# Linear attention, mixture of experts and a gated layer on one core: the order of the recurrence's products changed

## The chip, the core and the metric

The kernel runs on one core of a Trainium2 chip. Its engines are TensorE (PE in the profile; its weight loads are shown apart as PEld), VectorE (DVE), ScalarE (ACT), GpSimd (POOL) and SyncE (SP, which here only issues transfers). The metric is the device time of one execution in microseconds, the median of several runs.

## The reference, cut to what matters

Three stages follow one another: a gated linear recurrence (attention), a layer of eight experts of which each token takes one, and a dense gated layer.

```python
# attention: batch 4, heads 8, 768 steps, head size 48
state = f[:, :, t, :, None] * state + einsum('bhd,bhe->bhde', k[:, :, t], v[:, :, t])
y[:, :, t] = einsum('bhd,bhde->bhe', q[:, :, t], state)      # f = sigmoid(f_logit)
# experts: 3072 tokens of 384, 8 experts of width 1024
logits = x @ w_gate + modality_bias[modality_id]
e_idx = argmax(logits, axis=1);  probs = softmax(logits)
out[mask] = gate_w[mask, None] * (maximum(x[mask] @ w1[e], 0) @ w2[e])
# gated layer of width 1536
return (sigmoid(x @ w_gate) * (x @ w_val)) @ w_out
```

## The kernel before

**Tiles.** The recurrence is cut into chunks of 128 steps. With 6 chunks and 4 batches there are 24 tiles (NT); tile i belongs to chunk i // 4 and batch i % 4, and holds all 8 heads. A loop over i from 0 to NT + 1 writes the code of several tiles in one pass: the products of tile i, the outputs of tile i - 1, the routing of tile i - 2, and the preparation of tiles i + 2 and i + 3. The schedule is written by hand (`tc.manual_schedule()`): each engine works through its instructions in the order in which this code issues them, and waits on semaphores where it needs another's result.

**The products of one pass on PE,** under the names that the profile gives to their results:

- `ktr` (line 957): four transposes of the keys of tile i. The whole array is used, 128 rows by 128 columns.
- `a` (line 969): eight products of keys and queries of tile i. Each uses 48 rows of one half of the array's rows (64 by 128); two lie side by side. DVE masks them into `am` (line 975).
- `c` (line 923): eight sums of the log gates of tile i + 2. Each uses 64 columns (128 by 64); two lie side by side. ACT makes `r` and `g` from them.
- `xtok` (line 1047): four products that turn the output of tile i - 2 into token order and give the router's logits. Whole array.
- `u` (line 987): eight products for the state's update in tile i, 128 by 64. DVE adds them to `ss` (lines 997 and 999).
- `yT` of line 1015: four products of the queries of tile i - 1 with the state, whole array. Tiles of the first chunk have none. It is called yS below.
- `yT` of line 1021: eight products of `am` and the values of tile i - 1, 128 by 64, into the same accumulation. It is called yA below. ACT copies the result to memory (line 1026).

So the array is used in three shapes: whole (F), split by rows (R: only `a`), split by columns (C: `c`, `u`, yA). A float32 product shows as two MATMUL records in the trace. In the order before, one full pass reads F R C F C F C.

**Routing.** The tiles are routed in groups (ROUTE): 0 to 3, 4 to 7, 8 to 11, 12 to 15, 16 and 17, 18 to 21, 22 and 23. When the last tile of a group has gone through `xtok`, the generator `route_a` issues the steps on DVE from logits to the one-hot choice `oh`. One pass later `att_r` issues the `rank` products on PE, which count tokens per expert, and then `route_pos` on DVE: six small steps and, for each tile, one `row` and one `place` (lines 307 and 309), here called marks. `put_table` multiplies the marks on PE and adds the result to a table on DVE (line 334). DVE's steps of these generators are issued one at a time by `tick()` between other work, or all at once by `drain()`.

**Before, a pass after the rank products** (`to_put`) the code drains the marks and then issues the `put` products, in passes 7, 11, 15 and 19. After pass 19 the routing of tiles 16 and 17 gives the tables of the first two expert slots: `early_tables` on DVE, `put` and `take` on PE in pass 21, a gather of rows, and two expert slots in float32 (`slot32`), of which the first begins in pass 25.

**Buffers.** PSUM tiles rotate: three for `a` and `c`, two (tag "o") for `u` and `yT`, two (tag "t") for `ktr` and `xtok`, one (tag "lg") for `rank`, `put` and `take`. Every fourth pass from the third on (CONV) and the pass behind it also convert a piece of the last layer's weights, on ACT and DVE.

Of the kernel before, what the change touches and what calls it, by code (L numbers as in the profile page):

```python
# [10 lines left out]
F32 = mybir.dt.float32  # L11
# [11 lines left out]
P = 128  # L23
B, H, S, D = 4, 8, 768, 48
NCH = S // P
NT = B * NCH
NTOK = B * S
DM = H * D
E = 8
# [12 lines left out]
ROUTE = ((0, 4), (4, 4), (8, 4), (12, 4), (16, 2), (18, 4), (22, 2))  # L42
CUM = len(ROUTE) % 2
CONV = (3, 7, 11, 15)
GROUP = (0, 6, 1, 2)
STAGED = (3, 7)
PADS = (320, 160, 352, 96)
# [13 lines left out]
def kernel(  # L61
# [167 lines left out]
    def drain():  # L229
        while chains:  # L230
            tick()
# [11 lines left out]
    def route_a(logits_ps, bias, n, to):  # L243
        shp = [P, n, E]
        lg = small.tile(shp, F32, tag="lg", name="lg")
        nc.vector.tensor_tensor(out=lg, in0=logits_ps, in1=bias, op=ALU.add)
        yield
        mx = small.tile([P, n], F32, tag="mx", name="mx")
        nc.vector.tensor_reduce(out=mx, in_=lg, axis=AX.X, op=ALU.max)
        yield  # L250
        nc.vector.tensor_tensor(out=lg, in0=lg, in1=bc3(mx, shp, 2), op=ALU.subtract)
        ez = small.tile(shp, F32, tag="ez", name="ez")
        nc.scalar.activation(out=ez, in_=lg, func=AF.Exp)
        yield
        sc = small.tile(shp, F32, tag="sc", name="sc")
        w8b = bc3(w8, shp, 1)
        nc.vector.scalar_tensor_tensor(out=sc, in0=lg, scalar=0.0, in1=w8b, op0=ALU.is_ge, op1=ALU.mult)
        yield
        first = small.tile([P, n], F32, tag="first", name="first")
        nc.vector.tensor_reduce(out=first, in_=sc, axis=AX.X, op=ALU.max)  # L260
        yield
        oh = small.tile(shp, BF16, tag="oh", name="oh", bufs=3)
        nc.vector.tensor_tensor(out=oh, in0=w8b, in1=bc3(first, shp, 2), op=ALU.is_equal)
        to.update(oh=oh, ez=ez)
        yield

    def route_rank(oh, c, n, count=False):
        ps = ps_t.tile([P, n + count, E], F32, tag="lg", name="rank", bufs=1)
# [53 lines left out]

    marks = []

    def put_table():

        ps = ps_t.tile([HI, 2, P], F32, tag="lg", name="put", bufs=1)
        steps = [(half, row, place) for row, place in marks for half in range(2)]
        marks.clear()
        for n, (half, row, place) in enumerate(steps):  # L330
            nc.tensor.matmul(
                out=ps[:, half], lhsT=row[:, half], rhs=place, start=(n == 0), stop=(n == len(steps) - 1)
            )
        nc.vector.tensor_tensor(out=table, in0=table, in1=ps, op=ALU.add)
# [11 lines left out]
    def route_cum(oh, c, c_new, n):  # L346
        if n > 2:
            total = small.tile([P, E], F32, tag="total", name="total")
            nc.vector.tensor_reduce(out=total, in_=oh.rearrange("p n e -> p e n"), axis=AX.X, op=ALU.add)
            yield  # L350
            nc.vector.tensor_tensor(out=cum[c_new], in0=cum[c], in1=total, op=ALU.add)
            yield
        for j in range(n if n <= 2 else 0):
            nc.vector.tensor_tensor(out=cum[c_new], in0=cum[c if j == 0 else c_new], in1=oh[:, j], op=ALU.add)
            yield
# [650 lines left out]
                at = slice(64 * j, 64 * j + D)  # L1006
                nc.scalar.copy(out=s_blk[b][at, :, at], in_=s_sum[b][at])

    def att_y(i):
        c, b = i // B, i % B  # L1010
        (am, _), qT, vt = st.pop(("am", i)), st.pop(("qT", i)), st.pop(("v", i))
        ps = ps_o.tile([P, 4, P], F32, tag="o", name="yT")
        if c:
            for pr in range(4):
                nc.tensor.matmul(
                    out=ps[:, pr, :], lhsT=s_blk[b][:, pr, :], rhs=qT[:, pr, :], start=(pr == 0), stop=False
                )
        for pr in range(4):
            for j in range(2):
                h = 2 * pr + j  # L1020
                nc.tensor.matmul(
                    out=ps[64 * j:64 * j + 64, pr, :], lhsT=vt[:, h * D:h * D + 64], rhs=am[:, 4 * j + pr, :],
                    start=(c == 0 and pr == 0), stop=(pr == 3),
                )
        yT = ap2.tile([P, 4, P], F32, tag="yT", name="yT")
        nc.scalar.copy(out=yT, in_=ps)
        st["yT", i] = yT
# [35 lines left out]
    def att_r(i):  # L1063

        drain()
        first_i, n = group_of[i]
        c = ROUTE.index((first_i, n)) % 2
        got = st.pop(("oh", first_i))
        oh = got["oh"]
        rank = route_rank(oh, c, n, i == NE - 1)  # L1070
        steps = (
            route_pos(oh, rank, n, first_i, late_at(first_i, n)),
            route_cum(oh, c, 1 - c, n), route_weight(got["ez"], st["rows", first_i], n),
        )
# [12 lines left out]
    def general(flag):  # L1087
        with tc.If(flag != 0), ExitStack() as gctx:
# [53 lines left out]
            with tc.For_i(0, NTOK, P) as r0:  # L1142
# [22 lines left out]
                    nc.tensor.matmul(out=lg[:, 0], lhsT=xt[:, c, :], rhs=wn[:, c, :], start=(c == 0), stop=(c == 2))  # L1165
                got = {}
                run(route_a(lg, bi, 1, got))
                oh, ez = got["oh"], got["ez"]
# [72 lines left out]
        for _ in steps:  # L1241
            tick()

    to_store = due = to_put = None
    for i in range(NT + 2):
        routed = due
        due = i - 2 if i >= 2 and sum(group_of[i - 2]) == i - 1 else None
# [7 lines left out]
            load_v(i + 3)  # L1255
        if to_store is not None and to_store != NE - 1:
            store_rows(to_store)
        if i < NT:
            att_k(i)
            att_a(i)  # L1260
        if to_put and to_put < NE - 1:
            drain()
            put_table()
        if i == NE + 3:
            put_table()
        if i + 2 < NT:
            prep_c(i + 2)
            prep_e(i + 2)
        if i == NE + 3:
            tabs["ids"] = take_table(tabs["esel"], "eids").rearrange("p (t s) -> p t s", t=2)  # L1270
        if routed is not None and routed < NE - 1:
            att_r(routed)
        if i < NT:
            att_m(i)
        if i == NE + 2:
            drain()
            store_rows(NE - 1)
        tick()
        if i + 3 < NT:
            prep_l(i + 3)  # L1280
        if i in CONV:
            convert_mask()
        if i == NT + 1:
            slot_0 = slot32(w0, early_x[0], hooks_0, early_cur[0])
            next(slot_0)
        if 0 <= i - 2 < NT:
            att_x(i - 2)
            if i >= NT - 1:
                drain()
        if i == NT:  # L1290
            att_r(NT - 3)
            drain()
            to_store = NT - 3
        if i == NT + 1:
            next(slot_0)
            next(slot_0)
        if i < NT:
            state = att_u(i)
            if i == 0:
                keep_warm(1)  # L1300
        if 0 <= i - 1 < NT:
            att_y(i - 1)
        if i == NT - 1:
            gps = ps_t.tile([1, P], F32, tag="lg", name="gps", bufs=1)
            nc.tensor.transpose(gps, gm1, ident)
# [12 lines left out]
        to_put = routed  # L1318
# [448 lines left out]
```

## Time and profile before

| what | value |
|---|---|
| median of 3 runs | 879.3 us (875.5 to 879.44) |
| the profiled execution | 878.71 us, span 877.0 us |
| PE busy | 853.0 us (97%) of the span |
| DVE, ACT, POOL busy | 476.8 us (54%), 389.2 us (44%), 249.8 us (28%) |
| mean granted clock of TensorE | 0.991 of full speed |
| attention, passes 2 to 24 | about 21.7 to 164.8 us of the span |
| float32 expert slots, then experts | to about 212 us, then to about 418 us |
| gated layer | to the end |

PE counts as busy while any of its products is in flight, and that time is modelled, so 97% doesn't mean that it works at its peak: what a run of products costs is read from where it starts and where the next one starts.

### The profile page before, as it was taken

The numbers are of one execution on the slowest core, as the hardware profiler recorded it, in microseconds if no ns is written. First come the engines' busy times: TensorE is split into PE (matmuls) and PEld (weight loads), VectorE is DVE, ScalarE is ACT, GpSimd is POOL, SyncE is SP. The second block draws the span as 40 slices with busy tenths as digits, with TensorE's granted clock in tenths as the row PEclk, the third lists the DMA queues.
The fourth block names the chain that finished last, engine by engine and source line by source line (L and its number), as shares of the span: only waits on it lengthen the run. The fifth ranks groups of instructions, "written<-read, shape, count | busy, mean of one in ns | idle before, by whom it ended". The sixth has DMA issues, their size and how long they took to land.

```text
span 877.0 us, 15315 instructions
## 1 busy us (share of the span) xinstructions
PE 853.0 (97%) x5802; PEld 762.9 (87%) x5802; DVE 476.8 (54%) x1036; ACT 389.2 (44%) x804; POOL 249.8 (28%) x321
## 2 busy tenths in 40 slices
PE   7999999999999999999999999999999999999995
PEld 6888888777999999999888888888888888888885
DVE  5777778475987979976335334333423433442221
ACT  5866675225866656656432322232322332223222
POOL 5744443113445665564630200020020001002002
PEclk8999999999999999999999999999999999999998
DMA  9566653864989979976202021011012002000000
GB/s 324 177 219 232 217 171 123 332 242 149 336 302 327 330 270 321 333 260 226 80 10 64 27 47 35 1 55 37 18 46 46 19 1 64 10 0 37 1 1 36
DMA packets 52273, 121.15 MB, mean 138 GB/s; under 512 B 21018, under 2 KB 33318, under 8 KB 52192
## 3 DMA queue, kind: packets, MB, share of 16 engines
q1 hardware_dynamic: 47200, 105.10, 35.6%
q0 software_dynamic: 4992, 15.00, 4.8%
q8 instruction: 47, 0.77, 0.4%
q14 instruction: 34, 0.28, 0.1%
HBM read 96.44 MB, written 20.11 MB: 133 GB/s over the span
## 4 chain that ended last, share of the span: by engine, by line
PE 69%; DVE 4%; issue 1%; ACT 1%; POOL 0%; POOLq 0%; DVEq 0%; ACTq 0%
PE gv L1595 11%; PE gv L1596 11%; PE gv L1594 11%; PE y L735 8%; PE o L1619 6%; PE o L1617 6%; PE o L1618 6%; PE h L659 3%; PE h L656 3%; PE h L657 3%; DVE cvt L850 2%; DVE al L389 1%; DVE hl L663 1%; PE xT L403 0%; DVE bl L389 0%
## 5 line engine op out<-in xcount | busy, mean ns | idle before, releaser
L1605 DVE TENSOR_TENSOR sg<-sg,gv 128x256 f32<-128x256 f32 (+1 forms) x145 | 60.2, 415 | 209.3 <-PE gv L1596 209.3
L1606 ACT CAST gh<-sg 128x256 fp32r<-128x256 f32 (+1 forms) x145 | 58.7, 405 | 191.6 <-DVE sg L1605 191.6
L1625 POOL DMA_INDIRECT out_dram<-raw,tok x24 | 23.6, 984 | 375.5 <-ACT raw L1622 369.3
L1607 DVE TENSOR_TENSOR gl<-sg,gh 128x256 fp32r<-128x256 f32 (+1 forms) x145 | 64.3, 443 | 68.2 <-ACT gh L1606 68.2
L1604 ACT ACTIVATE sg<-gv 128x256 f32<-128x256 f32 (+1 forms) x145 | 55.2, 381 | 94.7 <-PE gv L1596 92.6
L393 POOL DMA_INDIRECT xg<-xd,ids x24 | 36.5, 1523 | 62.9 <-PE xT L403 38.9
L662 ACT ACTIVATE hh<-h 128x256 fp32r<-128x256 f32 x80 | 30.9, 386 | 42.7 <-PE h L659 42.0
L663 DVE SCALAR_TENSOR_TENSOR hl<-h,hh 128x256 fp32r<-128x256 f32 x80 | 33.3, 419 | 21.8 <-ACT hh L662 18.2
L1596 PE MATMUL gv<-oddh,al 128*128 128x512 f32 (+1 forms) x120 | 44.3, 369 | 0.0
L1595 PE MATMUL gv<-oddl,ah 128*128 128x512 f32 (+1 forms) x120 | 44.3, 369 | 0.0
L1594 PE MATMUL gv<-oddh,ah 128*128 128x512 f32 (+1 forms) x120 | 44.1, 367 | 0.0
L1596 PE MATMUL gv<-oddh,bl 128*128 128x512 f32 x108 | 42.5, 394 | 0.0
L1596 PE MATMUL gv<-evenh,bl 128*128 128x512 f32 x108 | 42.5, 393 | 0.0
L1595 PE MATMUL gv<-oddl,bh 128*128 128x512 f32 x108 | 42.4, 393 | 0.0
L1595 PE MATMUL gv<-evenl,bh 128*128 128x512 f32 x108 | 42.4, 393 | 0.0
L945 POOL TENSOR_TENSOR qT<-kq,g 128x512 f32<-128x512 f32 x19 | 24.4, 1283 | 62.9 <-ACT g L935 47.8
L1596 PE MATMUL gv<-evenh,al 128*128 128x512 f32 x108 | 42.3, 391 | 0.0
L1595 PE MATMUL gv<-evenl,ah 128*128 128x512 f32 x108 | 42.2, 391 | 0.0
L1594 PE MATMUL gv<-evenh,ah 128*128 128x512 f32 x108 | 42.0, 389 | 0.0
L1594 PE MATMUL gv<-evenh,bh 128*128 128x512 f32 x108 | 42.0, 389 | 0.0
L1594 PE MATMUL gv<-oddh,bh 128*128 128x512 f32 x108 | 42.0, 389 | 0.0
L975 DVE TENSOR_TENSOR am<-a,causal 128x512 f32<-128x512 f32 x48 | 31.2, 683 | 12.5 <-PE a L969 12.5
(365 smaller groups left out, 2487.8 us busy)
## 6 DMA issues: line engine op xcount, KB each, us to landing
raw<-in_w_dram SPq DMA_DIRECT2D x48, 768.0 KB, 5.8
kq<-in_att_kq_dram SPq DMA_DIRECT2D x24, 512.0 KB, 5.4
cvr<-in_w_glu_dram SPq DMA_DIRECT2D x14, 768.0 KB, 7.4
raw<-wd SPq DMA_DIRECT2D x7, 768.0 KB, 5.3
f<-in_att_fv_dram SPq DMA_DIRECT2D x24, 200.0 KB, 5.6
v<-in_att_fv_dram SPq DMA_DIRECT2D x24, 200.0 KB, 2.5
x<-yd SPq DMA_DIRECT2D x12, 386.0 KB, 3.4
xd<-rows SPq DMA_DIRECT2D x5, 772.0 KB
```

The costliest lines, as they stand in the source:

```text
L663: nc.vector.scalar_tensor_tensor(out=hl, in0=ps, scalar=0.0, in1=hh, op0=ALU.max, op1=ALU.subtract)
L735: nc.tensor.matmul(out=ps, lhsT=lhs[:, ts], rhs=rhs[:, fs], start=(g == 0 and part == 0), stop=(g == 7 and part == 2))
L1594: nc.tensor.matmul(out=ps[:, ns], lhsT=hi[:, sl], rhs=xh[:, c, ns], start=(c == 0), stop=False)
L1595: nc.tensor.matmul(out=ps[:, ns], lhsT=hi[:, sl], rhs=xl[:, c, ns], start=False, stop=False)
L1596: nc.tensor.matmul(out=ps[:, ns], lhsT=lo[:, sl], rhs=xh[:, c, ns], start=False, stop=(c == 2))
L1604: nc.scalar.activation(out=sg[:, sl], in_=pss[0][:, to], func=AF.Sigmoid)
L1605: nc.vector.tensor_tensor(out=sg[:, sl], in0=sg[:, sl], in1=pss[1][:, to], op=ALU.mult)
L1606: nc.scalar.copy(out=gh[:, sl], in_=sg[:, sl])
L1607: nc.vector.tensor_tensor(out=gl[:, sl], in0=sg[:, sl], in1=gh[:, sl], op=ALU.subtract)
L1617: nc.tensor.matmul(out=ps, lhsT=gh[:, ts], rhs=hi[:, fs], start=(f == 0), stop=False)
L1618: nc.tensor.matmul(out=ps, lhsT=gh[:, ts], rhs=lo[:, fs], start=False, stop=False)
L1619: nc.tensor.matmul(out=ps, lhsT=gl[:, ts], rhs=hi[:, fs], start=False, stop=(f == 11))
```

## The change

The pass is written in another order. `att_y` is cut in two: `att_ys` issues yS early in the pass, and `att_y` issues yA later. On PE a full pass becomes `ktr`, yS, `xtok` (F), then `a` (R), then yA, `c`, `u` (C). The `rank`, `put` and `take` products stand between `xtok` and `a`. The ACT work behind `c` (`prep_e`, `prep_l`) moves to the end of the pass. `put_table` is called in passes 9, 13, 17 and 20 (PUT) and no longer drains the marks; in pass 20 it takes a buffer of tag "t". The exponent of the logits leaves `route_a` and is issued with the rank products (`route_exp`).

```diff
+PUT = (9, 13, 17, 20)
...
         nc.vector.tensor_tensor(out=lg, in0=lg, in1=bc3(mx, shp, 2), op=ALU.subtract)
-        ez = small.tile(shp, F32, tag="ez", name="ez")
-        nc.scalar.activation(out=ez, in_=lg, func=AF.Exp)
         yield
...
+    def route_exp(lg, n):
+        ez = small.tile([P, n, E], F32, tag="ez", name="ez")
+        nc.scalar.activation(out=ez, in_=lg, func=AF.Exp)
+        return ez
...
-    def att_y(i):
+    def att_ys(i):
         c, b = i // B, i % B
-        (am, _), qT, vt = st.pop(("am", i)), st.pop(("qT", i)), st.pop(("v", i))
+        qT = st.pop(("qT", i))
         ps = ps_o.tile([P, 4, P], F32, tag="o", name="yT")
         if c:
             for pr in range(4):
...
+        st["y", i] = ps
+
+    def att_y(i):
+        c = i // B
+        (am, _), vt, ps = st.pop(("am", i)), st.pop(("v", i)), st.pop(("y", i))
...
         if i < NT:
             att_k(i)
-            att_a(i)
-        if to_put and to_put < NE - 1:
-            drain()
-            put_table()
-        if i == NE + 3:
-            put_table()
-        if i + 2 < NT:
-            prep_c(i + 2)
-            prep_e(i + 2)
-        if i == NE + 3:
-            tabs["ids"] = take_table(tabs["esel"], "eids").rearrange("p (t s) -> p t s", t=2)
-        if routed is not None and routed < NE - 1:
-            att_r(routed)
-        if i < NT:
-            att_m(i)
...
+        if 0 <= i - 1 < NT:
+            att_ys(i - 1)
...
             att_x(i - 2)
             if i >= NT - 1:
                 drain()
+        if i in PUT:
+            put_table(**({"tag": "t"} if i == PUT[-1] else {}))
+        if i == NE + 3:
+            tabs["ids"] = take_table(tabs["esel"], "eids").rearrange("p (t s) -> p t s", t=2)
...
+        if routed is not None and routed < NE - 1:
+            att_r(routed)
+        if i < NT:
+            att_a(i)
+            att_m(i)
...
+        tick()
...
+        if 0 <= i - 1 < NT:
+            att_y(i - 1)
+        if i + 2 < NT:
+            prep_c(i + 2)
         if i < NT:
             state = att_u(i)
             if i == 0:
                 keep_warm(1)
-        if 0 <= i - 1 < NT:
-            att_y(i - 1)
+        if i + 2 < NT:
+            prep_e(i + 2)
+        if i + 3 < NT:
+            prep_l(i + 3)
```

On PE, one full pass in the middle of the recurrence before the change reads as follows (each row is a line, the result and its inputs, and the shape; the eight products of `a` stand one by one, and six are left out).

```order
L957 MATMUL ktr<-ident,kT 128x128 x4
L969 MATMUL a_1007<-qT,kT 128x128
L969 MATMUL a_1008<-qT,kT 128x128
...
L923 MATMUL c<-causal,nl 64x128 x8
L1047 MATMUL xtok<-wr,yT 128x104 x4
L987 MATMUL u<-v,kt 64x48 x8
L1015 MATMUL yT<-qT,s_140 128x128 x4
```

Behind it comes yA of line 1021. After the change a full pass on PE reads as follows; the lines have moved down by four or more.

```order
L961 MATMUL ktr<-ident,kT 128x128 x4
L1019 MATMUL yT<-qT,s_139 128x128 x4
L1056 MATMUL xtok<-wr,yT 128x104 x4
L973 MATMUL a_901<-qT,kT 128x128
L973 MATMUL a_902<-qT,kT 128x128
...
L1030 MATMUL yT<-am,v 64x128 x8
L927 MATMUL c<-causal,nl 64x128 x8
L991 MATMUL u<-v,kt 64x48 x8
```

The three whole-array runs stand together, and so do the three runs that are split by columns.

On DVE, the place in question is pass 19, after the change: `ss` is the state's update, which waits for `u` of this pass; `row` and `place` are the marks of tiles 12 to 15; `lg` to `oh` are the routing steps of tiles 16 and 17, whose `rank` products stand on PE directly behind `u` of pass 19.

```order
L1001 TENSOR_TENSOR ss_144<-ss_144,u 128x192
L311 TENSOR_SCALAR row<-iota_hi,hi 128x192
L1003 TENSOR_TENSOR ss_144<-ss_144,g 128x192
L313 TENSOR_SCALAR place<-iota_lo,lo,iota_t 128x128
...
L247 TENSOR_TENSOR lg<-lgs,bias_all 128x16
L250 TENSOR_REDUCE mx<-lg 128x2
L252 TENSOR_TENSOR lg<-lg,mx 128x16
L256 SCALAR_TENSOR_TENSOR sc<-lg,w_97 128x16
L259 TENSOR_REDUCE first<-sc 128x2
L262 TENSOR_TENSOR oh<-w_97,first 128x16
```

Left out are three more rows of `row` and three of `place`. Before the change the eight marks stood ahead of the table's add and of `am` of pass 19, and only the routing steps stood behind the state's update:

```order
L309 TENSOR_SCALAR place<-iota_lo,lo,iota_t 128x128
L334 TENSOR_TENSOR table<-table,put 96x256
L975 TENSOR_TENSOR am<-a_2119,causal 128x512
L975 TENSOR_TENSOR am<-a_2120,causal 128x512
L1051 TENSOR_REDUCE lgs<-xtok 128x8
L997 TENSOR_TENSOR ss_144<-ss_144,u 128x192
L246 TENSOR_TENSOR lg<-lgs,bias_all 128x16
L999 TENSOR_TENSOR ss_144<-ss_144,g 128x192
```

On PE around the same place, after the change: the last run of pass 19, the first and last `rank` product for tiles 16 and 17, then pass 20 with yS, `xtok`, the marks of tiles 12 to 15, and, behind `c`, the `put` of pass 21.

```order
L991 MATMUL u<-v,kt 64x48 x8
...
L276 MATMUL rank<-oh,ones 128x8
...
L283 MATMUL rank<-ebase,ones 128x16
L1019 MATMUL yT<-qT,s_140 128x128 x4
L1056 MATMUL xtok<-wr,yT 128x104 x4
L335 LDWEIGHTS row
...
L927 MATMUL c<-causal,nl 64x128 x8
L335 LDWEIGHTS row
```

Before, pass 20 had `a` and `c` directly behind `rank`, so `am` of tile 20 came earlier on DVE; now yS, `xtok` and `put` stand between.

## Rows read from the trace of the kernel before

**Rows 1.** Busy time by stretch: passes 5 to 18, then 19 to 24.
```profile
37.53:132.40 94.87, 94.11 (x1226) 80.98 (x1224) 73.71 (x191) 62.69 (x134) 43.58 (x48) 1.00 0.62 204
132.40:164.76 32.36, 31.11 (x378) 27.35 (x376) 23.22 (x100) 15.05 (x33) 8.97 (x13) 1.00 0.60 230
```
**Rows 2.** Timeline of PE, one full pass: start us, length us, instruction.
```profile
85.54 0.65 PE L957 MATMUL ktr<-ident,kT 128*128 128x128 f32 x4
86.12 1.16 PE L969 MATMUL a<-qT,kT 48*128 48x128 f32 x16
87.21 1.09 PE L923 MATMUL c<-causal,nl 128*64 128x128 f32 x16
88.24 1.14 PE L1047 MATMUL xtok<-wr,yT 128*128 128x104 f32 x8
89.31 0.67 PE L987 MATMUL u<-v,kt 128*64 128x48 f32 x16
89.91 1.16 PE L1015 MATMUL yT<-qT,s 128*128 128x128 f32 x8
91.00 1.09 PE L1021 MATMUL yT<-am,v 128*64 128x128 f32 x16
92.02 0.66 PE L957 MATMUL ktr<-ident,kT 128*128 128x128 f32 x4
```
**Rows 3.** Timeline of PE in pass 1, without xtok and yS.
```profile
19.38 1.10 PE L923 MATMUL c<-causal,nl 128*64 128x128 f32 x16
20.30 0.62 PE L987 MATMUL u<-v,kt 128*64 128x48 f32 x16
20.75 1.06 PE L1021 MATMUL yT<-am,v 128*64 128x128 f32 x16
21.75 0.66 PE L957 MATMUL ktr<-ident,kT 128*128 128x128 f32 x4
```
**Rows 4.** Timeline of PE in pass 20, without ktr and u.
```profile
142.37 1.14 PE L1047 MATMUL xtok<-wr,yT 128*128 128x104 f32 x8
143.34 1.08 PE L1015 MATMUL yT<-qT,s 128*128 128x128 f32 x8
144.35 1.09 PE L1021 MATMUL yT<-am,v 128*64 128x128 f32 x16
```
**Rows 5.** Timeline of PE: put in pass 11 and, much later, in slot 0.
```profile
79.55 1.25 PE L331 MATMUL put<-place,row 128*96 128x128 f16 x8
187.29 0.83 PE L331 MATMUL put<-raw 128*96 128x128 f16 x12
```
**Rows 6.** Timeline of DVE in pass 19: first and last mark, state's update, routing.
```profile
133.22 0.27 DVE L307 TENSOR_SCALAR row<-iota_hi,hi 128x192 f16<-128x192 bf16 x1
134.62 0.30 DVE L309 TENSOR_SCALAR place<-iota_lo,lo,iota_t 128x128 f16<-128x128 bf16 x1
137.99 0.35 DVE L997 TENSOR_TENSOR ss<-ss,u 128x192 f32<-128x192 f32 x1 [0.42 <-PE u L987]
139.47 0.17 DVE L263 TENSOR_TENSOR oh<-w,first 128x16 bf16<-128x16 f32 x1
```
**Rows 7.** Timeline of DVE in passes 20 and 21.
```profile
142.72 0.16 DVE L291 CAST di<-df 128x2 int32<-128x2 f32 x1
145.36 0.23 DVE L417 TENSOR_TENSOR ecmp<-rank,iota_b 128x88 f32<-128x88 f32 x1
148.24 0.41 DVE L334 TENSOR_TENSOR table<-table,put 96x256 f32<-96x256 f32 x1
```
**Rows 8.** Timeline of PE: take in pass 21.
```profile
148.70 0.61 PE L341 MATMUL take<-esel,table 96*128 96x4 f32 x4 [0.79 <-DVE table L334]
```
**Rows 9.** Timeline of PE in the expert stage: the longest wait there.
```profile
256.71 0.44 PE L735 MATMUL y<-ah,hl 128*128 128x384 f32 x1 [1.84 <-DVE hl L663]
```
**Rows 10.** Busy time by stretch, right behind that wait (PEclk is third from the end).
```profile
257.40:260.70 3.30, 3.30 (x15) 3.30 (x14) 3.27 (x6) 0.56 (x2) 2.63 (x3) 0.50 0.86 299
```
**Rows 11.** Timeline of ACT in the pass of rows 2.
```profile
85.65 0.59 ACT L1026 COPY yT<-yT 128x512 f32<-128x512 f32 x1 [0.39 <-PE yT L1021]
```

More of the change, by code (lines that the diff above doesn't have):

```diff
@@ L263, in route_a @@
         nc.vector.tensor_tensor(out=oh, in0=w8b, in1=bc3(first, shp, 2), op=ALU.is_equal)
-        to.update(oh=oh, ez=ez)
+        to.update(oh=oh, lg=lg)
         yield
+    def route_exp(lg, n):
+        ez = small.tile([P, n, E], F32, tag="ez", name="ez")
+        nc.scalar.activation(out=ez, in_=lg, func=AF.Exp)
+        return ez
     def route_rank(oh, c, n, count=False):
@@ L323, with put_table @@
     marks = []
-    def put_table():
-        ps = ps_t.tile([HI, 2, P], F32, tag="lg", name="put", bufs=1)
+    def put_table(**home):
+        ps = ps_t.tile([HI, 2, P], F32, name="put", **(home or {"tag": "lg", "bufs": 1}))
         steps = [(half, row, place) for row, place in marks for half in range(2)]
@@ L1068, in att_r @@
         got = st.pop(("oh", first_i))
-        oh = got["oh"]
+        oh, ez = got["oh"], route_exp(got["lg"], n)
         rank = route_rank(oh, c, n, i == NE - 1)
@@ L1072, in att_r @@
             route_pos(oh, rank, n, first_i, late_at(first_i, n)),
-            route_cum(oh, c, 1 - c, n), route_weight(got["ez"], st["rows", first_i], n),
+            route_cum(oh, c, 1 - c, n), route_weight(ez, st["rows", first_i], n),
         )
@@ L1167, in general @@
                 run(route_a(lg, bi, 1, got))
-                oh, ez = got["oh"], got["ez"]
+                oh, ez = got["oh"], route_exp(got["lg"], 1)
                 rank = route_rank(oh, CUM, 1)
@@ L1242, in ticking @@
             tick()
-    to_store = due = to_put = None
+    to_store = due = None
     for i in range(NT + 2):
@@ L1257 @@
             store_rows(to_store)
+        if i == NE + 3:
+            put_table()
         if i < NT:
             att_k(i)
-            att_a(i)
-        if to_put and to_put < NE - 1:
-            drain()
-            put_table()
-        if i == NE + 3:
-            put_table()
-        if i + 2 < NT:
-            prep_c(i + 2)
-            prep_e(i + 2)
-        if i == NE + 3:
-            tabs["ids"] = take_table(tabs["esel"], "eids").rearrange("p (t s) -> p t s", t=2)
-        if routed is not None and routed < NE - 1:
-            att_r(routed)
-        if i < NT:
-            att_m(i)
[L1275 to L1282, printed above, removed]
+        if 0 <= i - 1 < NT:
+            att_ys(i - 1)
         if i == NT + 1:
@@ L1289 @@
                 drain()
+        if i in PUT:
+            put_table(**({"tag": "t"} if i == PUT[-1] else {}))
+        if i == NE + 3:
+            tabs["ids"] = take_table(tabs["esel"], "eids").rearrange("p (t s) -> p t s", t=2)
         if i == NT:
@@ L1293 @@
             to_store = NT - 3
+        if routed is not None and routed < NE - 1:
[3 more added lines that the diff above has]
+            att_m(i)
+        if i == NE + 2:
+            drain()
+            store_rows(NE - 1)
+        tick()
         if i == NT + 1:
@@ L1300 @@
                 keep_warm(1)
-        if 0 <= i - 1 < NT:
-            att_y(i - 1)
+        if i + 2 < NT:
+            prep_e(i + 2)
+        if i + 3 < NT:
+            prep_l(i + 3)
+        if i in CONV:
+            convert_mask()
         if i == NT - 1:
@@ L1317 @@
             to_store = routed if routed != NT - 3 else None
-        to_put = routed
         if routed == NE - 1:
```

## The prediction

> **What bounds the kernel now.** I first read the busy time by stretch. In passes 5 to 18 of the recurrence PE is busy for 94.11 of 94.87 us, DVE for 73.71, ACT for 62.69, and the DMA share is 0.62 [rows 1]. Busy PE time is modelled, so I then read PE's timeline of one full pass, for where each run of products starts [rows 2]. From one start to the next: `ktr` 0.58, `a` 1.09, `c` 1.03, `xtok` 1.07, `u` 0.60, yS 1.09, yA 1.02, together 6.48 us. No row there shows idle time with a releaser: PE sets the pace, and what a run costs is in these steps. The reader is to see that equal work costs unequal time by its neighbours. In pass 1 `c` stands ahead of another run of its own shape and takes 0.92 instead of 1.03; `u`, with its shape on both sides, takes 0.45 instead of 0.60; yA, behind its shape, 1.00 instead of 1.02 [rows 3]. In pass 20 `xtok` is followed by its shape and takes 0.97 instead of 1.07; yS, behind it, 1.01 instead of 1.09 [rows 4]. So leaving a run for another shape costs some 0.10, and entering one 0.08 in a whole-array run and 0.02 to 0.04 in a run split by columns.
>
> **The recurrence's runs.** Worked out with these differences, a pass after the change is: `ktr` 0.58 - 0.10 = 0.48; yS 1.09 - 0.08 - 0.10 = 0.91; `xtok` 1.07 - 0.08 = 0.99; `a` 1.09, unchanged; yA 1.02 - 0.11 = 0.91; `c` 1.03 - 0.02 - 0.11 = 0.90; `u` 0.60 - 0.04 = 0.56. The sum is 5.84, 0.64 less. Passes 5 to 18 are 14 such passes: **9.0 us less**. Passes 2 to 4 have no yS, and `u` already stood ahead of yA: 6.48 - 1.09 - 0.13 = 5.26 before, 5.84 - 0.91 = 4.93 after, 3 x 0.33 = **1.0 less**. Two joins have no row of their own: `ktr` to yS, and yA to `c`. If they cost as much as a change of shape does, 14 x 0.18 = 2.5 and 17 x 0.13 = 2.2 us come back; nothing in the rows suggests a gain above what I took. I take the rows of the same shapes, since the shape is all that those runs share with their neighbours.
>
> **Does another engine become the bound?** DVE's 73.71 us now go into 94.87 - 9.0 - 2.1 = 83.8 us, 88%; ACT's are 75% [rows 1]. DVE has 5.3 us per pass on average against 5.84. Passes with marks and a conversion of weights run over that, and their neighbours have room; PE takes `am` only a pass later. The new tight place is yT's buffer: yS of a pass needs the buffer of the `yT` before, after ACT's copy. That copy ends at 85.65 + 0.59 = 86.24, 0.70 us after the run behind yA has begun [rows 2, 11]; after the change `c`, `u` and `ktr`, 1.94 us, lie between, which leaves 1.24 us. Loads have two passes of lead; I cost them at nothing, hidden behind those passes.
>
> **The table's products.** A put of eight products takes 1.25 us in pass 11, since PE waits for marks that DVE issues just ahead; twelve that wait for nothing take 0.83, or 0.07 each [rows 5]. Two passes later the marks are long done, so eight cost 0.56. Three of the four puts (passes 7, 11 and 15, now 9, 13 and 17) save 0.69 each: **2.1 less**. The fourth belongs to the next part. The exponent with the rank products frees ACT of a wait on DVE that no row of PE's timeline hangs on: nothing.
>
> **The end of the recurrence, where the change takes back.** I count from the start of `ktr` of pass 19. Without the drain ahead of `put`, the eight marks of tiles 12 to 15 and the six routing steps of tiles 16 and 17 now all stand on DVE behind the state's update, which needs `u`. `u` ends at 5.9. From the state's update to the end of `oh` DVE took 139.47 + 0.17 - 137.99 = 1.65, and the marks take some 1.6 (133.22 to 134.62 and one more step) [rows 6]: `oh` is ready at 9.2, while PE stands ready for `rank` at 5.85. PE waits **3.4 us** where it waited for nothing. Behind `rank` come yS 0.9, `xtok` 0.9, `put` 0.6 and only then `a` of tile 20, done at 13.0. Its two `am` take DVE to 14.3; from there to the end of `ecmp` it took 145.36 + 0.23 - 142.72 = 2.9 [rows 7], so the marks of 16 and 17 let `put` of pass 21 start at 17.2. PE got there at 14.9: a second wait, 2.3 us. Behind `ecmp` the table's add ended 3.1 us later (148.24 + 0.41 - 145.59) [rows 7], and `take` follows it at 20.2. Before, `take` stood at 148.70 - 132.40 = 16.3 [rows 1, 8]. So it comes 3.9 later. The products from there to slot 0 are the same but for a join or two, some 0.3 less. Sum for passes 19 to 24: **3.6 more**. Its lower bound is 0, if DVE gets through the marks ahead of the update after all; above 3.9 nothing in the rows points.
>
> **The clock.** [...] Half clock for 3.3 us costs 1.65 if it falls on the runs ahead of `am` of tile 20, and nothing if it falls on the second wait; with no row to choose, I take the middle, **0.85 more**.
>
> Sum against the profiled execution's own 878.7: - 9.0 - 1.0 - 2.1 + 3.6 + 0.85 = **871.0 us**. That execution lies 0.6 below the median of 879.3. What follows the recurrence is paced by its own products and by loads that they release, and moves forward as it is.
>
> **Rivals.**
> *The end costs less.* If DVE gets its marks in ahead of the state's update, or the clock stays up: 871.0 - 3.6 - 0.85 = 866.5 at most. For it: DVE idles 0.42 us ahead of that update [rows 6]. Against it: an engine doesn't pass an instruction that waits, and the marks stand behind.
> *The two unseen joins cost as a change of shape does,* or DVE at 88% holds PE up now and then: 871.0 + 2.5 + 2.2 = 875.7.
> *Joining runs brings nothing.* [...] Then only the puts are saved and the end still pays: 878.7 - 2.1 + 3.6 + 0.85 = 881.0, slower. It decides once a join saves less than (3.6 + 0.85 - 2.1) / 14 = 0.17 a pass. Against it stand the differences of 0.10 and 0.08 that [rows 3, 4] show for just such neighbours. [...]
> *yT's copy comes too late.* ACT's copy of `xtok` stands ahead of it and waits for DVE's reduction. If DVE is late enough in every pass, yS waits, and the pass loses what it gained. It decides at a wait of 0.64 a pass, a copy 1.9 us late; at 1.2 a pass, 871.0 + 14 x 1.2 = 887.8. For it: DVE at 88%. Against it: 1.24 us of room, and a mean load that fits.
>
> **How the numbers follow.** A change of 0.5%, some 4.4 us, is about what a measurement of this kernel can tell from none; faster by that is below 874.9. Forecast (868 to 873.5) 0.62; the end costs less (to 866.5) 0.13; joins or DVE (to 875.7) 0.17, half of it beyond 874.9 at most; joining brings nothing 0.04; the copy 0.04. Nearly all of the chance is on one side. The range from 866.5 to 875.7 leaves out the last two and the edges. Faster 0.87, same 0.08, slower 0.05.
>
> **What would show it.** In the profile after: full passes of 5.8 to 5.9 us between starts of `ktr`; `ktr` 0.48, yS 0.91, `c` 0.90; puts in passes 9, 13 and 17 with no wait; an idle time of some 3.4 us ahead of `rank` in pass 19, and some 2.3 ahead of `put` in pass 21, each ended by DVE; `take` some 20 us behind `ktr` of pass 19; perhaps a stretch of half clock in pass 20. The forecast is wrong if yS shows idle time ended by ACT, if passes of 6.4 us remain, or if the expert stage does not simply begin 8 us earlier.

## The result and the profile after

The changed kernel takes 887.47 us (median of six runs, 884.04 to 890.56) against 877.86 us (median of six, 875.48 to 879.64). The ratio is 1.0111, with an interval from 1.0075 to 1.0148: it is **slower by 9.6 us**, where 7.7 us less was forecast, and the time lies outside the range. The profiled execution took 890.56 us, with a span of 888.9.

I compared the two traces by stretch first. This is the busy time of the kernel after in passes 2 to 4, 5 to 18, 19 to the first product of slot 0, and the rest (length, then PE, PEld, DVE, ACT and POOL; the granted clock of TensorE is third from the end).

```profile
23.68:38.38 14.70, 14.70 (x232) 13.87 (x229) 9.62 (x17) 13.11 (x28) 9.51 (x14) 1.00 0.59 168
38.38:135.61 97.23, 91.06 (x1228) 85.81 (x1224) 77.87 (x186) 63.78 (x136) 49.52 (x48) 0.93 0.62 204
135.61:177.81 42.20, 32.99 (x381) 30.23 (x377) 25.64 (x99) 16.32 (x36) 11.07 (x15) 0.92 0.52 197
177.81:888.86 711.05, 694.39 (x3810) 625.78 (x3808) 359.31 (x717) 286.49 (x589) 176.31 (x195) 1.00 0.35 117
```

Passes 2 to 4 took 15.79 us before (21.75 to 37.53 by the starts of `ktr`) and take 14.70: 1.1 less, as forecast. Passes 5 to 18 take 97.23 instead of 94.87 [rows 1]: 2.4 more, where 11.1 less was forecast. Passes 19 to 24 take 42.20 instead of 32.36 [rows 1]: 9.8 more, where 3.6 and 0.85 for the clock were forecast. The rest is 1.2 shorter than before, and pass 2 starts 1.9 later. This last part is not the change's: over the kernels measured here pass 2 started between 19.5 and 23.7 us, at 19.75 and 23.46 in two that have the same instructions up to there (experiments 6 and 8). A difference of 2 us between two single executions can come from there, so the stretches are compared below beside the medians. The sum, -1.1 + 2.4 + 9.8 - 1.2 + 1.9 = 11.8, is the difference of the two spans. The reader is to see where to look: PE is now idle for 6.2 us of passes 5 to 18 (0.8 before), and its clock there is 0.93 (1.00 before) [rows 1].

Where nothing is waited for, the joined runs do what was said of them. PE's timeline in pass 12:

```profile
84.48 0.66 PE L961 MATMUL ktr<-ident,kT 128*128 128x128 f32 x4
84.97 1.06 PE L1019 MATMUL yT<-qT,s 128*128 128x128 f32 x8
85.87 1.04 PE L1056 MATMUL xtok<-wr,yT 128*128 128x104 f32 x8
86.83 1.16 PE L973 MATMUL a<-qT,kT 48*128 48x128 f32 x16
87.93 1.09 PE L1030 MATMUL yT<-am,v 128*64 128x128 f32 x16
88.85 1.04 PE L927 MATMUL c<-causal,nl 128*64 128x128 f32 x16
89.72 0.62 PE L991 MATMUL u<-v,kt 128*64 128x48 f32 x16
90.28 0.66 PE L961 MATMUL ktr<-ident,kT 128*128 128x128 f32 x4
```

From start to start: `ktr` 0.49, yS 0.90, `xtok` 0.96, `a` 1.10, yA 0.92, `c` 0.87, `u` 0.56, together 5.80 us where 5.84 was forecast and 6.48 stood before [rows 2]. The loss is in waits. PE's waits from 20 to 178 us (us in total, times, the longest):

```profile
PE rank L277 <- DVE oh L262: 6.0, 4, 1.7
PE rank L276 <- DVE oh L262: 3.7, 1, 3.7
PE xT L732 <- DMA xg<-xd,eids: 2.7, 2, 1.4
PE take L345 <- DVE table L338: 1.5, 1, 1.5
PE put L335 <- DVE ecmp L421: 1.3, 1, 1.3
```

The first row is the one that I had not foreseen: in passes 6, 10, 14 and 18 the rank products wait for `oh`, the last of the six routing steps that DVE takes in the pass ahead. DVE's timeline from the end of pass 8 to `oh` in pass 9:

```profile
64.66 1.76 DVE L950 SCALAR_TENSOR_TENSOR kT<-r,kq 128x512 f32<-128x512 f32 x1
...
67.32 1.16 DVE L868 SCALAR_TENSOR_TENSOR raw<-raw 128x768 f32<-128x768 f32 x1
68.40 0.18 DVE L1060 TENSOR_REDUCE lgs<-xtok 128x8 f32<-128x32 f32 x1
...
70.83 1.42 DVE L1003 TENSOR_TENSOR ss<-ss,g 128x192 f32<-128x192 f32 x1
...
72.26 0.68 DVE L950 SCALAR_TENSOR_TENSOR kT<-r,kq 128x512 f32<-128x512 f32 x1
72.86 0.50 DVE L262 TENSOR_TENSOR oh<-w,first 128x32 bf16<-128x32 f32 x1
```

The second half of the weights' conversion (L865 and L868) ends pass 8 on DVE. Behind it `lgs` starts the routing at 68.40, and the six steps then stand one by one between an addition to the table, two `am`, two state updates and `kT`: 5.0 us from `lgs` to the end of `oh`, of which the seven routing instructions are about 1.6. The same place before the change, on DVE and then on PE:

```profile
65.63 0.96 DVE L864 SCALAR_TENSOR_TENSOR raw<-raw 128x768 f32<-128x768 f32 x1
...
68.63 0.19 DVE L1051 TENSOR_REDUCE lgs<-xtok 128x8 f32<-128x32 f32 x1 [0.81 <-PE xtok L1047]
...
71.92 0.19 DVE L263 TENSOR_TENSOR oh<-w,first 128x32 bf16<-128x32 f32 x1
```

```profile
73.94 0.19 PE L273 MATMUL rank<-oh,before 128*128 128x32 bf16 x1
```

Count both from the start of `ktr` of pass 9 (64.75 before, 62.66 after). The conversion ended 1.8 us behind it and now ends 5.8 behind it; `oh` ended at 7.4 and now ends at 10.7; PE stood ready for `rank` at 9.2 and now does at 9.0. So PE, whose pass 9 is shorter by the order but now holds a put, asks for `oh` hardly earlier: it is DVE that is 3.3 us later. Before, DVE waited for PE in every pass, as in the 0.81 us above; after, it waits for nothing from 57.0 us to the end of `oh`. Passes 13 and 17 read alike; in pass 5 `oh` is 1.7 us later, and PE asks 1.0 earlier.

PE comes for `oh` right behind `xtok` of pass 10:

```profile
73.41 0.18 PE L277 MATMUL rank<-oh,before 128*128 128x32 bf16 x1 [1.74 <-DVE oh L262]
...
73.64 1.85 PE L973 MATMUL a<-qT,kT 48*128 48x128 f32 x16
75.42 1.97 PE L1030 MATMUL yT<-am,v 128*64 128x128 f32 x16
```

`a` takes 1.85 and yA 1.97 us behind that wait instead of 1.16 and 1.09. The windows behind the waits of passes 10 and 18, of `rank` in pass 19 and of `take` show why; the granted clock in them is 0.50:

```profile
73.94:77.35 3.41, 3.41 (x34) 3.19 (x33) 1.59 (x5) 0.26 (x2) 0.19 (x2) 0.50 0.97 383
131.97:135.37 3.40, 3.40 (x42) 3.40 (x40) 1.34 (x5) 0.91 (x2) 0.00 (x0) 0.50 0.52 177
145.62:149.03 3.41, 3.41 (x19) 3.41 (x19) 1.12 (x5) 0.01 (x1) 0.00 (x0) 0.50 0.02 5
159.27:162.68 3.41, 3.41 (x34) 3.25 (x32) 1.29 (x2) 0.58 (x1) 0.00 (x0) 0.50 1.01 344
```

Behind the wait of pass 14 it is 0.50 for 6.82 us (101.25 to 108.07). Behind the shorter wait of pass 6 (0.80 us) the clock stayed at 1.00 (47.40 to 51.00).

At the end `take` stands 22.0 us behind `ktr` of pass 19 (157.61 - 135.61; 20.2 forecast, 16.3 before [rows 8]), and slot 0's first product 20.2 behind `take`'s start instead of 16.1. PE's timeline, then POOL's:

```profile
157.61 0.61 PE L345 MATMUL take<-esel,table 96*128 96x4 f32 x4 [1.55 <-DVE table L338]
...
172.49 0.55 PE L732 MATMUL xT<-ident,xg 128*128 128x128 f32 x3 [1.27 <-DMA xg<-xd,eids]
```

```profile
164.13 1.26 POOL L949 TENSOR_TENSOR qT<-kq,g 128x512 f32<-128x512 f32 x1 [8.95 <-issue]
...
165.70 1.27 POOL L397 DMA_INDIRECT xg<-xd,eids  x1 [0.17 <-issue]
```

The rows that `take` names are asked for 7.5 us after `take` has ended (158.2), because the gather stands behind `qT` of tile 23 on POOL's queue.

### The profile page after: what moved, and what is told of

Same layout as the page of the kernel before. It is cut to its first block, busy times and chain, and to the rows that moved or that the text cites. A ratio compares the mean times of both kernels' runs of the same rounds, so it can differ in the third digit from the quotient of the medians.

```text
span 888.9 us, 15294 instructions
## 1 busy us (share of the span) xinstructions
PE 852.0 (96%) x5802; PEld 771.9 (87%) x5802; DVE 483.2 (54%) x1036; ACT 390.3 (44%) x804; POOL 257.0 (29%) x321
## 4 chain that ended last, share of the span: by engine, by line
PE 66%; DVE 5%; issue 1%; ACT 1%; POOL 0%; DMA 0%; POOLq 0%; DVEq 0%; ACTq 0%
PE gv L1605 11%; PE gv L1606 11%; PE gv L1604 11%; PE y L739 7%; PE o L1629 6%; PE o L1627 6%; PE o L1628 6%; PE h L663 3%; PE h L660 3%; PE h L661 2%; DVE cvt L854 2%; DVE bl L393 1%; DVE al L393 1%; DVE hl L667 1%; PE xT L407 0%
## 5 line engine op out<-in xcount | busy, mean ns | idle before, releaser
L949 POOL TENSOR_TENSOR qT<-kq,g 128x512 f32<-128x512 f32 x19 | 27.0, 1423 | 73.5 <-issue 54.7
```

## The experiments

**Theory A**: `rank` waits because `oh` is late by DVE's order of work, and the half clock follows from these waits. **B**: DVE has too much to do, whatever its order. **C**: `oh` is late because DVE's steps take longer while POOL works beside them. **D**, for the end: the gather stands behind `qT`. All times are medians; the kernel before took 878.8 to 878.9 beside them.

**1. Routing at once.**

```
-            if i >= NT - 1:
+            if i >= NT - 1 or due is not None:
                 drain()
```

> One change to the kernel after: when the last tile of a group of four has its xtok product (passes 5, 9, 13, 17), all six steps of its routing up to oh are issued to DVE at once, ahead of am, instead of one by one between am, the state update and kT. PE's order is untouched. Theory A (rank waits for oh because oh stands last behind a DVE backlog, and each such wait brings a stretch of half clock): rank(6), (10), (14), (18) start without a wait (7.1 us less: 1.08 and three of 2.02) and the half-clock stretches at 74, 101 and 132 us go (3.41 + 6.82 + 3.41 us at half speed, 6.8 us lost), so about 14 us less than after: 873 to 875 us. The wait in pass 19 (3.87) stays. Theory B (DVE has too much to do in these passes whatever its order): am, then kT, are late in place of oh; PE waits as long at ktr, a or yA one pass later, and the time stays at 886 to 890.

Measured: **874.98 us**, 0.9965 of before [0.9946, 0.9984], 12.5 less than after. DVE's timeline in pass 9, then the busy time in passes 5 to 18:

```profile
66.37 0.18 DVE L1060 TENSOR_REDUCE lgs<-xtok 128x8 f32<-128x32 f32 x1
...
67.70 0.19 DVE L262 TENSOR_TENSOR oh<-w,first 128x32 bf16<-128x32 f32 x1
```

```profile
37.31:121.48 84.17, 84.02 (x1229) 79.66 (x1225) 75.46 (x186) 63.68 (x135) 49.02 (x48) 1.00 0.69 230
```

`oh` now ends 1.5 us behind the start of `lgs`. No wait of `rank` is left in these passes, the clock is 1.00, and the stretch takes 84.17 us: 10.7 less than before, where 11.1 was forecast. DVE does the same 186 instructions in it, so B is wrong. `kT` still takes 0.92 us on average (0.99 in after, 0.68 alone), and costs nothing.

**2. The conversion one pass earlier.**

```
-CONV = (3, 7, 11, 15)
+CONV = (2, 6, 10, 14)
```

> One change to the kernel after: the four weight conversions start one pass earlier (mask and the first DVE half in passes 2, 6, 10, 14, the second DVE half, 1.3 to 2.0 us of DVE, at the end of passes 3, 7, 11, 15 instead of 4, 8, 12, 16). It no longer stands directly ahead of the passes in which a group's routing is issued; the order of the routing's steps is untouched. Theory A (the backlog that makes oh late is the conversion's second half): oh comes about 2 us earlier, rank's waits of 2.02 go, and with them the half clock: 873 to 877 us. Theory A2 (the place of oh behind am, state update and kT is enough by itself): rank still waits 0.5 us or more in each of the four passes; 880 to 888. Rival: the conversion now lies beside the marks, and the puts in passes 9, 13 and 17 wait 1 us or more each instead.

Measured: 879.29 us, 1.0015 [0.9994, 1.0036]: 8 less than after, but neither expectation. `rank` waits 0.37 in each pass, since `oh`, still behind `kT`, takes 1.26 us beside POOL's `qT`; and a new wait of up to 0.5 stands ahead of yS, on ACT. DVE's timeline:

```profile
70.01 1.26 DVE L262 TENSOR_TENSOR oh<-w,first 128x32 bf16<-128x32 f32 x1
```

Counted as above, `oh` ends at 9.7 instead of 10.7 us, and the wait at yS puts `rank` off from 9.0 to 9.4: together that leaves 0.37 of the 1.74, less than the 1.1 that `oh` itself loses here. The puts did not wait. Passes 5 to 18 take 88.00.

**3. Products ahead of `rank` that nobody reads.**

```
+HEAT = {6: 2, 10: 4, 14: 4, 18: 4}
...
         if routed is not None and routed < NE - 1:
+            heat(HEAT[i])
             att_r(routed)
```

> The kernel after with products that nobody reads put on PE directly ahead of rank: two (pass 6) and four (passes 10, 14, 18) of 128x256 fp32 on a PSUM buffer of their own turn (about 0.43 us each at full clock). PE computes while it would wait; oh comes no earlier, and rank starts about when it did. Theory A, part 2 (the half clock follows from the idle time): the stretches of half clock at 74, 101 and 132 us are gone and some 6.8 us with them: 880 to 883 us; rank waits 0.1 to 0.4 us behind the products. Rival (the half clock has another cause than idle time, for instance the kind of products that precede): the stretches stay and the time is that of after, 887 to 890. Should the waits themselves be most of the loss, it shows here as what is left: 882 against 878 of the kernel before.

Measured: **881.27 us**, 1.0028 [1.0012, 1.0044]. Passes 5 to 18:

```profile
36.41:127.57 91.16, 90.78 (x1257) 84.55 (x1253) 77.92 (x186) 63.59 (x135) 49.38 (x48) 1.00 0.64 215
```

The clock is 1.00, and 6.1 of the 97.23 us are gone. PE still spends the time of the waits, on nothing. So of the 13.1 us between after (97.23) and experiment 1 (84.17), about **6.1 are half clock and 7.0 the waits**. The split is good to about a microsecond: the stretches at 0.50 in these passes are 13.6 us long, which is 6.8 lost, and the listed waits are 6.0.

**4. The limit of f on DVE instead of POOL.**

```
-        (nc.vector if i < 5 else nc.gpsimd).tensor_scalar(
+        nc.vector.tensor_scalar(
```

> One change to the kernel after: the limit of the forget logits (f, 1.2 to 1.9 us on POOL a pass) runs on DVE (0.35 to 0.37 us each where DVE does it in passes 0 to 4). POOL has about 22 us less work in passes 5 to 18, DVE 14 x 0.36 = 5.0 us more. Theory C (oh is late because DVE's steps are stretched while POOL works: kT 1.7 instead of 0.68, ss 1.4 instead of 0.36, conversion 2.0 instead of 0.96): the steps beside f lose their stretch, rank's waits shrink from 2.02 to under 1, half-clock stretches go: 874 to 880 us. Theory A (order and conversion decide): DVE has 0.36 us more in each pass ahead of oh and rank waits about as long as before, 2.0 +- 0.5; the time stays within 3 us of after.

Measured: 887.43 us, 1.0101 [1.0061, 1.014], as after. POOL's busy time in passes 5 to 18 falls from 49.52 to 24.05, the conversion no longer takes 2.02 (at most 0.96), and `rank` still waits up to 1.5 us, 5.2 in all. C, as far as `f` goes, is not the cause. POOL's `qT` stays beside DVE here (64.06 to 65.33 and 70.46 to 71.73), and two steps on the way to `oh` pay for it:

```profile
64.10 1.44 DVE L1003 TENSOR_TENSOR ss<-ss,g 128x192 f32<-128x192 f32 x1
70.51 1.27 DVE L256 SCALAR_TENSOR_TENSOR sc<-lg,w 128x32 f32<-128x32 f32 x1
```

Alone they take 0.36 and 0.19. That is 2.2 us on a DVE that waits for nothing, against a wait of 1.5; in after `kT`, `ss` and `oh` of the lines above lose 2.5, against 1.7. So C, as far as `qT` goes, is a part of the lateness, and perhaps all of what makes it a wait; no run takes `qT` away.

**5. The puts and the exponent alone, in the order of before.**

```
-        if to_put and to_put < NE - 1:
-            drain()
-            put_table()
+        if i in PUT:
+            put_table(**({"tag": "t"} if i == PUT[-1] else {}))
```

> The kernel before with two parts of the change alone: the puts in passes 9, 13, 17 and 20 (no drain ahead of them), at before's place in the pass, and the exponent with the rank products. PE's order of products is before's. The prediction's terms: three puts that no longer wait (2.1 us less), nothing for the exponent: 876 to 878 us. Theory B (late puts and marks themselves crowd DVE and make oh late, whatever PE's order): rank waits as in after and the time is 884 or more. Theory A (oh is late because the new order asks for it about 3 us earlier in its pass, while DVE's order gives it no earlier): no wait of rank over 0.5 us in passes 6, 10, 14, 18.

Measured: 878.42 us, 0.9996 [0.9976, 1.0016]. No wait of `rank` in passes 6 to 18. These passes take 93.10 us, 1.8 less than before (2.1 forecast), and 1.1 come back at the end, where `rank` of pass 19 now waits 1.2. Without the new order, `oh` is early enough, but not for the reason in the expectation: PE asks for `rank` 2.70 us into pass 10 here, 2.50 in after, while `oh` ends 0.87 into it here, 4.19 in after. The time is just above the range expected, by what came back at the end.

**6. Routing at once in pass 19 too.** With experiment 1:

```
+            if i - 2 == NE - 1:
+                chains.insert(0, chains.pop())
+                tick(6)
```

> Experiment 1 (routing steps at once in passes 5, 9, 13, 17) and the same in pass 19: the steps of tiles 16 and 17 up to oh go ahead of the marks of tiles 12 to 15, which stood before them. Theory A: rank(19) starts without its wait of 3.7 to 3.9 us, the half clock behind it (131.3 to 134.8 us in experiment 1: yS 1.85 instead of 0.89, xtok 1.67 instead of 0.97) goes as well, 5.5 us in all, unless the chain from rank to the table (rank's end to take 13 us) is what sets the end: then take waits up to 4 us more. 869.5 to 873.5 us. Rival (the marks, now later, hold up put(20)): put waits 2 us or more, and 873 to 876.

Measured: **869.21 us**, 0.9907 [0.9876, 0.9938]: faster than both kernels. The wait of `rank` in pass 19 is gone; the passes to slot 0 take 37.0 us instead of 41.6. Put and take wait 1.7 and 1.2.

```profile
118.62:155.65 37.03, 31.43 (x379) 28.61 (x377) 25.16 (x99) 16.44 (x36) 10.93 (x15) 0.95 0.62 238
```

**7. The table's chain issued at the end of pass 19.** With experiment 6 (the put of pass 20 keeps its four tiles):

```
             prep_mul(i + 2)
+            if i == NE + 1:
+                drain()
             tick(3)
```

> Experiment 6, and all that follows rank(19) on DVE up to the columns of the table (d to eei, 26 steps of about 0.2 us) is issued at the end of pass 19 instead of one by one behind the reduce of xtok, the put's addition and am of pass 20, for which it stood still 3 us in experiment 1 (132.6 to 135.5 us). The put of pass 20 still takes four tiles. Theory A (DVE's order again, not its load): take waits under 1 us; 1.5 to 3 us less than experiment 6: 868 to 871. Rival (the chain's own length, about 8 us from rank's end, sets take): take waits as in experiment 6, within 1 us of it.

Measured: 872.23 us, 0.994 [0.992, 0.9959]: 3 more than experiment 6, of which the passes to slot 0 show 1.6 (38.67 for 37.03 us). `take` waits 0.35, as A had it, but the reduction of `xtok` now stands behind the chain, and `xtok` of the next pass waits for its PSUM buffer:

```profile
133.60 2.01 PE L1056 MATMUL xtok<-wr,yT 128*128 128x104 f32 x8 [1.88 <-DVE lgs L1060]
```

**8. The gather right behind `eids`.** With experiment 7:

```
             tabs["ids"] = take_table(tabs["esel"], "eids").rearrange("p (t s) -> p t s", t=2)
+            gather_x(NE * P, 0)
```

> Experiment 7, and the gather of the first early slot is issued on POOL directly behind the table's columns (eids) instead of behind qT(23), which waits for c's exponents of pass 21. Theory D (xT waits for rows that were asked for late, because the gather stands behind qT on POOL's queue): the gather is issued 3 to 6 us earlier, xT's waits (1.1 to 3 us in all) go; 1 to 3 us less than experiment 7. Rival (the DMA itself is as late, behind the pieces of the weights that are loaded in the same stretch): xT waits as long; no change.

Measured: 869.83 us, 0.9899 [0.9873, 0.9924]: 2.4 less than experiment 7, and 3.1 less in the passes to slot 0 (35.57 us). POOL issues the gather 1.5 us behind the start of `take` (139.95), and `xT` waits no more:

```profile
141.47 1.26 POOL L397 DMA_INDIRECT xg<-xd,eids  x1 [4.66 <-DVE eids L347]
```

D holds.

**9. Experiment 6 with that gather.**

> Experiment 6 (routing steps at once in passes 5, 9, 13, 17 and 19) with the gather of experiment 8 (directly behind eids on POOL), without experiment 7's issue of the table's chain. Theory D: the waits of xT for the gathered rows (1.8 and 1.3 us in experiment 6) go, nothing else moves: 866 to 868 us, passes 19 to the first early product 35 us instead of 37.0. Rival (the gather was not what held xT): 869, as experiment 6.

Measured: 869.0 us, 0.9883 [0.9836, 0.993], four runs from 864.83 to 871.54. `xT`'s waits are gone, yet the profiled run (871.19) gained little, 36.54 us to slot 0 for 37.03: put waits 2.80 instead of 1.69. One mark on DVE is why, with POOL's `qT` beside it from 133.70 to 134.97:

```profile
133.60 1.42 DVE L313 TENSOR_SCALAR place<-iota_lo,lo,iota_t 128x128 f16<-128x128 bf16 x1
```
In experiment 6 the same `place` took 0.31, though it started as far ahead of `qT` (131.59 and 131.70); there a later step of the chain, `ect`, took 0.69 instead of 0.17. So which step pays, and how much, does not show in the starts, and half clock follows the longer wait (0.50 from 136 to 140 us). That this is the whole spread of the four runs is argued, not shown: one of them has a profile.

**10. The chain in pass 20, behind `lgs`.** With experiment 9 (and the put of four tiles):

```
+            if i == NE + 2:
+                drain()
```

> Experiment 9, and the rest of the table's chain (d to eei) is issued in pass 20 directly behind the reduce of its xtok (lgs), ahead of the put's addition and am; in experiment 7 it stood ahead of lgs, and xtok of pass 21 waited 1.9 us for lgs to read its PSUM buffer. Theory A: put (1.7 us in experiment 6) and take (1.2) wait under 0.5 us each and xtok not at all: 1.5 to 2.5 us less than experiment 9, 864 to 866. Rival (am, now behind the chain, holds up a or yA of pass 21 by as much): within 0.7 us of experiment 9.

Measured: 869.71 us, 0.9895 [0.9859, 0.9931]. A fell here. The time is the rival's, but not its mechanism: `am` holds up neither `a` nor yA. Put and `xtok` wait no more (put 0.23), and `take` waits instead, for the second addition to the table, which stands behind `am`.

```profile
139.89 1.01 PE L345 MATMUL take<-esel,table 96*128 96x4 f32 x4 [3.24 <-DVE table L338]
```

`take` starts 11.6 us behind `rank` in experiments 8 and 10 alike (139.95 and 139.89, from 128.29 and 128.32). What lies between is DVE's marks, `qT`, `kT`, chain, two `am` and the additions to the table; where in it the wait shows is a matter of order. Both additions ahead of the `am` were not tried.

**11. The order alone**, with the puts and the exponent of before:

```
-        if i in PUT:
-            put_table(**({"tag": "t"} if i == PUT[-1] else {}))
+        if to_put and to_put < NE - 1:
+            drain()
+            put_table()
```

> The kernel after with its new order of products, but the puts one pass behind the routing with the drain ahead of them, as before (in passes 7, 11, 15, 19), and the exponent among the routing's steps. Theory A: the order alone makes rank wait for oh: 1 to 2 us in passes 6, 10, 14, 18 and the half clock behind it, as in after; each put waits besides for the marks that the drain issues, 1 to 3 us, since it now stands three products earlier in its pass than before: 890 to 896 us. Theory B (the late puts and the late exponent make oh late): no such wait of rank; 872 to 880 us.

Measured: 892.11 us, 1.0143 [1.009, 1.0196]. The time is A's; the waits are only in part. PE's waits from 20 to 180 us and ACT's from 36 to 140 us:

```profile
PE put L337 <- DVE place L315: 7.2, 4, 1.9
PE yT L1021 <- ACT yT L1037: 3.3, 4, 0.9
```

```profile
ACT ez L254 <- DVE lg L252: 4.5, 4, 1.1
```

The exponent, early on ACT, waits for DVE's `lg` and holds up the copy of yT, so PE stops at yS, and at `rank` only once (0.4); the drain stops it at the put. The new order meets a late DVE at whichever product comes first. Counted as in pass 9 above, the conversion ends at 4.75 us here (1.8 in experiment 5, 5.8 in after) and `oh` at 8.5 (7.9 and 10.7). So the new order alone makes DVE late, and the late marks, which cost nothing in the order before, add to it in this one.

**12. The waiting product moved.** `att_r(routed)` stands behind `prep_c(i + 2)` instead of ahead of `att_a(i)`:

```
-            tick(3)
+            tick(6 if routed is not None else 3)
```

> The kernel after with the waiting product moved instead of the awaited one: in passes 6, 10, 14, 18 the rank products stand behind c, between c and u, where PE comes 2.9 us later (a 1.09, yA 0.92, c 0.87) than now; DVE's order up to oh is that of after (oh still last, behind kT), three more of the routing's steps follow at the end of the pass. Theory A (the loss in passes 5 to 18 is the wait of rank, which is asked for up to 2.0 us too early, and the half clock behind it): the four waits are under 0.3 us, passes 5 to 18 take 84 to 86 us (97.2 in after, 84.2 in experiment 1), although rank now splits the run of products that are split by columns (0.1 to 0.3 us a time). The steps behind rank come later, so the wait in pass 19 may grow from 3.9 to 5 or 6 us: 874 to 878 us in all. Rival (DVE's backlog meets PE at the next thing it asks for, am or kT, wherever rank stands): passes 5 to 18 still take over 92 us.

Measured: 877.24 us, 0.9988 [0.9969, 1.0007]: 10 less than after. The wait in pass 19 did not grow (3.7). Passes 5 to 18:

```profile
37.31:122.51 85.20, 85.05 (x1229) 79.59 (x1225) 77.75 (x183) 63.68 (x136) 49.75 (x48) 1.00 0.67 227
```

`oh` comes as late as in after, `rank` 2.9 us later, and nothing waits. Moving either end of the dependence removes the loss.

## Why the prediction was wrong

**The step that failed** is the answer under "Does another engine become the bound?": that passes with marks and a conversion run over, that "their neighbours have room", and that PE takes `am` only a pass later. I asked when PE needs `am`, and not when it needs `oh`; and the neighbours had no room. The new order does not ask for `oh` much earlier (9.0 us behind the start of pass 9 instead of 9.2). It takes `u` last in the pass, 5.2 us into it (89.72 in the lines of pass 12) instead of 3.8 [rows 2], and on DVE the state's update waits for `u`, with `kT` and the conversion behind it. Together with the marks this keeps DVE full over two passes, and `oh`, at the end of that queue, ends 3.3 us later than before. That `u` is the link is read from the order of the lines; that the new order delays DVE, and that `oh`'s place and the time at which PE asks for it decide, is shown by experiments 11, 1 and 12. What share the steps lengthened beside POOL's `qT` have stays open (experiment 4). The trace of before had what I did not read: `oh` ended only 1.8 us ahead of `rank`, behind the conversion's second half. One rival names DVE at 88%, "now and then", without the value or the pass, and prices it by the joins, at 875.7. The time that I gave for the rival of yT's copy, 887.8, is near what was measured by luck: in after PE waits nowhere for that copy.

**The runs: right.** 5.80 us a pass for 5.84; 1.1 less in passes 2 to 4 for 1.0; and with `oh` early, 84.17 in passes 5 to 18 for 83.8. The two joins without a row of their own bring their gain in full. Against the rival by which joining brings nothing stand `ktr`, yS and `xtok`: all three use the whole array, and joined they take 0.49, 0.90 and 0.96 instead of 0.58, 1.09 and 1.07.

**The puts and the exponent: right, nearly.** 1.8 for 2.1 (experiment 5). I costed the exponent at nothing; in this order, left ahead of the routing's end, it holds up the copy of yT, with 3.3 us of waits in four passes (experiment 11). No run moves the exponent alone.

**The end: the mechanism right, the size too small.** `rank` waits 3.7 (3.4 forecast) behind exactly the marks that I named, and put 1.3 (2.3). `take` comes 1.8 later than forecast. Of that, put is 1.0 late (153.82 - 135.61 = 18.2 for 17.2): the half clock behind `rank`, for which I had half the price in the clock's term, makes `a` of tile 20 end some 1.9 late, and the way from there to `ecmp` is shorter than forecast. The other 0.8 is one step of the chain between put's marks and `take`, which takes 0.17 in experiments 9 and 10 and 1.01 here, beside POOL's `qT` (153.78 to 155.06):

```profile
154.07 1.01 DVE L430 TENSOR_TENSOR_SCAN ect<-full 128x8 f32<-128x8 f32 x1
```

The way from `take` to slot 0, which I had at 0.3 less, costs 4.1 more: the gather behind `qT` and the half clock behind `take`. Moving that gather took 2.4 back in experiment 8, and no more than 0.2 in experiment 9.

**The clock: a term too few.** I gave one wait 0.85 us, the middle between nothing and half of the 3.3 us at 0.50 of [rows 10]; no run shows that term. What the trace of after shows in its place is five stretches at 0.50 in the recurrence, 20.4 us long in all (the four windows above and the 6.82 of pass 14). By an estimate from these lengths half of it, some 10 us, is lost.

With DVE's order mended, the change gives 869.0 to 872.2 us (experiments 6 to 10), inside the range given. That does not bear the forecast out: these kernels lack the wait of `rank` in pass 19, which the sum counts, and by its own terms they should take 866.5. Experiment 1, which keeps that wait, takes 874.98 for 871.0. What stays open is how far the end can still be shortened, and what the spread of experiment 9 comes from.

## What to carry to other kernels

When an engine's products are put into a new order, list each value that they read, by how much it stood ready early, and what the other engine's queue waits for ahead of it: a product that moves back (here `u`) delays all that stands behind its result there. A mean load of 88% says nothing about one value that stands last in the fullest pass. Issue short chains that another engine waits for at once, ahead of work that is due a pass later, and price an idle time of PE with the slower products behind it: here 7.0 us of waits cost 13.1.

## What was not expected of the hardware

Some DVE steps took longer while POOL worked beside them: `ss` 1.42 us at 70.83 against 0.35, with POOL's `qT` from 70.71 to 72.03; `kT` up to 1.76 against 0.68, with `qT` from 64.39 to 65.87; `oh` 1.26 against 0.18 in experiment 2; `place` 1.42 against 0.31 in experiment 9. The `am`, whose one operand lies in PSUM, took 0.67 to 0.69 in all 48 records of after, and the reductions of the routing 0.16 to 0.20. POOL's line beside that `ss`:

```profile
70.71 1.32 POOL L949 TENSOR_TENSOR qT<-kq,g 128x512 f32<-128x512 f32 x1 [2.35 <-issue]
```

Over passes 5 to 18 DVE's `kT` took 0.99 us on average (0.74 before) and `place` 0.57 (0.31 before). In experiment 1 this cost nothing (`kT` 0.92, `place` 0.57, no wait). In after `kT`, `ss` and `oh` on the way to pass 10's `rank` took 2.5 us longer together, and that `rank` waited 1.74; what part of the wait this made stays open (experiment 4).

The clock did not answer to every wait. In the expert stage of after PE's timeline has the same wait as before (1.83 us for 1.84) [rows 9], and the window behind it has a granted clock of 1.00 instead of 0.50 [rows 10]:

```profile
269.78 0.44 PE L739 MATMUL y<-ah,hl 128*128 128x384 f32 x1 [1.83 <-DVE hl L667]
```

```profile
270.40:273.70 3.30, 3.30 (x26) 3.30 (x26) 3.27 (x6) 1.68 (x2) 2.69 (x3) 1.00 0.78 264
```
